# A two-layer SiLU block on one core: which queue loads the first slab of w1, and in what order the first tiles of x are transposed

## The chip, the cores and the metric

The kernel runs on one core of a Trainium2 chip. The metric is the device time of one execution in microseconds; the median of three runs of the kernel before is 124.64 us (124.32 to 124.81). Its profile is of one further execution on the same core.

## The reference

`x` is 2048 x 640, `w1` 640 x 1728, `w2` 1728 x 640, all bf16. The kernel computes

```python
h = jnp.einsum("bsd,df->bsf", x, w1)
h = _silu(h)
out = jnp.einsum("bsf,fd->bsd", h, w2)
```

## The kernel before

**Tiling.** The 640 rows of w1 are five slabs of 128 (index k), held in SBUF as `w1s[:, k, :]`. The 1728 columns are 13 blocks of 128 and a last one of 64. x is needed with its 640 columns on the partitions, so it is loaded by transposing DMAs into `xT[:, k, :]`; a "tile" here is 128 columns of x (one k) by one chunk of 512 rows, and there are four chunks. A block of h for one chunk is the sum over the five k of a matmul of slab k's block with tile k. Each such matmul is issued as a pair of 64 columns of weights (`step`, L183 to L187), whose two halves stand beside each other in the array; a pair is called a part. ScalarE applies SiLU as it moves a finished block from PSUM to SBUF (L179). The second product, with w2, follows when all of h is there.

**The opening.** For the first chunk, the first eight blocks have one PSUM bank each. So the loop order is turned round there: for each k in turn, one sweep over the eight blocks (`sweep`, L192 to L195; eight parts each). Sweep k needs slab k of w1 (its first 1024 columns, 256 KB) and tile k of x, and nothing else, so that TensorE can begin when the first slab and the first tile are there and the others arrive behind. The fifth sweep (L208 to L211) finishes the blocks. After it come the other five blocks of the first chunk, whose columns are loaded separately as `ld_rest` and `ld_rest2` (L156, L157), then the three other chunks, whose 15 one-tile transposing loads (L163) and the loads of w2 follow on the same queue.

**Ahead of the opening** TensorE runs dummy matmuls on a zeroed tile `z` (L129 to L138): 13 over the full array and then one pair of 64 columns, each 256 wide. Their result is overwritten.

**Queues.** The helper `early` (L98 to L109) moves an instruction ahead of the barrier at the program's head, at the end of what already stands there for the same engine, so that on each engine the order of the `early` calls is the order of issue. SyncE's order is written out by hand in L123 and L148 to L157: tiles 0 and 1 in one transposing load; the last three of slab 0's eight blocks; slab 1; slab 2; tile 2; slab 3; tiles 3 and 4 in one load; slab 4; the two loads of the remaining columns. ScalarE issues one load, the first five blocks of slab 0 (L124, `NA = 5`), and then warms up its SiLU table (L144). Each load has a semaphore of its own, and TensorE waits at the head of each sweep for the loads that it needs (L199, L205, L208), and once more inside sweep 0, at block 5, for the last three blocks (L202). All transposing loads are issued from SyncE.

Of the kernel before, what the change touches and what calls it, by code (L numbers as in the profile page):

```python
# [9 lines left out]
def bass_standalone__dense_activation_silu__prompt_kernel(  # L10
# [13 lines left out]
    P = 128  # L24
    NB = 8
    BANK = 512
    DT = D // P
    FT = F // P
    FL = F - FT * P
    SCH = 512  # L30
# [8 lines left out]
    pe, act, dve, pool, sp = nc.tensor, nc.scalar, nc.vector, nc.gpsimd, nc.sync  # L39

    with ExitStack() as es:
# [18 lines left out]
        def sem(name):  # L60
            s = es.enter_context(nc.semaphore(name))
            count[s.name if hasattr(s, "name") else name] = 0
            return [s, 0]

        def tick(ins, s, n=1):
            ins.then_inc(s[0], n)
            s[1] += n
            return (s, s[1])

        def wait(eng, *points):  # L70
            for pt in points:
                if pt is None:
                    continue
                s, v = pt
                key = (id(eng), id(s))
                if seen.get(key, 0) < v:
                    eng.wait_ge(s[0], v)
                    seen[key] = v
# [6 lines left out]
        def load(eng, out_ap, in_ap):  # L85
            s = sem(f"s_ld{n_dma[0]}")
            n_dma[0] += 1
            return tick(eng.dma_start(out=out_ap, in_=in_ap), s, 16)

        def turned(c0, c1, k0, k1):  # L90
            s = sem(f"s_tr{n_dma[0]}")
            n_dma[0] += 1
            return tick(sp.dma_start_transpose(
                out=xT[:, k0:k1, c0:c1], in_=xf[c0:c1, k0 * P:k1 * P]), s, 16)

        ET = mybir.EngineType

        def early(emit, engine, arrived=True):  # L98
            n = len(nc.main_func.blocks[0].instructions)
            r = emit()  # L100
            lst = nc.main_func.blocks[0].instructions
            new = lst[n:]
            del lst[n:]
            at = next(
                i for i, ins in enumerate(lst)
                if ins.opcode == ("EventSemaphore" if arrived else "Drain") and ins.engine == engine
            )
            lst[at:at] = new
            return r  # L109
# [2 lines left out]
        w2_v = w2[0:F0, :].rearrange("(ft p) d -> p ft d", p=P)  # L112

        NO = NB
        NA = 5
        CO = NO * P

        def slab(eng, k, f0=0, f1=NO):
            return load(eng, w1s[:, k, f0 * P:f1 * P], w1_v[:, k, f0 * P:f1 * P])

        ld_w1 = {}
        ld_t = {}
        ld_t[0] = ld_t[1] = early(lambda: turned(0, SCH, 0, 2), ET.SP, False)  # L123
        ld_w1[0] = early(lambda: slab(act, 0, 0, NA), ET.Activation, False)  # L124
        p_z = early(lambda: tick(dve.memset(z[:, :], 0.0), s_dve), ET.DVE, False)  # L125

        bank_free = [None] * NB
# [1 line left out]
        def dummies(n, w):  # L129
            for _ in range(n):  # L130
                for c0 in range(0, P, w):
                    pe.matmul(ps[c0:c0 + w, 3, 0:HB], lhsT=z[:, 0:w], rhs=z[:, :],  # L132
                              start=True, stop=True)

        def first_dummies():
            wait(pe, p_z)
            dummies(13, P)
            dummies(1, HC)  # L138

        p_warm = early(lambda: tick(pool.memset(warm[:, :], 0.0), s_pool), ET.Pool, False)  # L140
# [4 lines left out]

        early(warm_up, ET.Activation, False)

        ld_w1b = early(lambda: slab(sp, 0, NA, NO), ET.SP, False)  # L148
        ld_w1[1] = early(lambda: slab(sp, 1), ET.SP, False)
        ld_w1[2] = early(lambda: slab(sp, 2), ET.SP, False)  # L150
        ld_t[2] = early(lambda: turned(0, SCH, 2, 3), ET.SP, False)
        ld_w1[3] = early(lambda: slab(sp, 3), ET.SP, False)
        ld_t[3] = ld_t[4] = early(lambda: turned(0, SCH, 3, DT), ET.SP, False)
        ld_w1[4] = early(lambda: slab(sp, 4), ET.SP, False)
        CM = CO + 2 * P
        ld_rest = early(lambda: load(sp, w1s[:, :, CO:CM], w1_v[:, :, CO:CM]), ET.SP, False)  # L156
# [32 lines left out]
        def part(k, ft, c0, c1, start=False, stop=False):  # L189
            return step(ft, k, ft, c0, c1, start, stop)  # L190

        def sweep(k, c0, c1, *waits):  # L192
            wait(pe, *waits)
            for ft in range(NO):
                part(k, ft, c0, c1)  # L195

        def opening():
            first_dummies()
            wait(pe, ld_t[0], ld_w1[0])  # L199
            for ft in range(NO):  # L200
                if ft == NA:
                    wait(pe, ld_w1b)  # L202
                part(0, ft, 0, SCH, start=True)
            for k in range(1, DT - 1):
                sweep(k, 0, SCH, ld_w1[k], ld_t[k])  # L205

        early(opening, ET.PE)
        wait(pe, ld_w1[4], ld_t[4])  # L208
        for ft in range(NO):
# [198 lines left out]
```

## Time and profile before

| what | value |
|---|---|
| median of three runs (lowest, highest) | 124.64 us (124.32, 124.81) |
| span of the profiled execution | 123.84 us (123.8 on the page) |
| its distance to the median of the runs | 0.80 us |
| TensorE matmuls busy | 121.3 us, 98% of the span |
| TensorE weight loads busy | 58.9 us, 48% |
| ScalarE, VectorE, GpSimd busy | 38.8, 6.9, 0.3 us |
| DMA packets | 10.42 MB, mean 84 GB/s |

The profile has a page, which gives busy times, the chain of work that ended last, the costliest groups and the DMA issues, and a trace behind it that can be asked further: a timeline in order of time, the same for one engine, the transfers with the time from issue to landing, and busy times in stretches of the span. Engines are named PE (matmuls), PEld (weight loads, which overlap the matmuls), ACT (ScalarE), DVE (VectorE), POOL (GpSimd) and SP (SyncE); SPq and ACTq are the DMA issues of SyncE and ScalarE. Times count from the span's start. In a line such as "3.82 0.18 PEld L175 ... [0.42 <-DMA xT<-in_x_dram]" the first number is the start, the second the length of what is merged there, "x4" the number of instructions, and the bracket the idle time just before with what ended it. The profiled execution is one among several, and the runs differ among themselves by up to 0.5 us.

### The profile page before, as it was taken

The numbers are of one execution on the slowest core, as the hardware profiler recorded it, in microseconds if no ns is written. First come the engines' busy times: TensorE is split into PE (matmuls) and PEld (weight loads), VectorE is DVE, ScalarE is ACT, GpSimd is POOL, SyncE is SP. The second block draws the span as 40 slices with busy tenths as digits, with TensorE's granted clock in tenths as the row PEclk, the third lists the DMA queues.
The fourth block names the chain that finished last, engine by engine and source line by source line (L and its number), as shares of the span: only waits on it lengthen the run. The fifth ranks groups of instructions, "written<-read, shape, count | busy, mean of one in ns | idle before, by whom it ended". The sixth has DMA issues, their size and how long they took to land.

```text
span 123.8 us, 2298 instructions
## 1 busy us (share of the span) xinstructions
PE 121.3 (98%) x1056; PEld 58.9 (48%) x1057; DVE 6.9 (6%) x11; ACT 38.8 (31%) x67; POOL 0.3 (0%) x5
## 2 busy tenths in 40 slices
PE   8999999999999999999999999999999999999993
PEld 5345545545545545545544444444444444444452
DVE  0000000000000000000000022002200300222001
ACT  4000985555555555555530011001100200110110
POOL 0000000000000000000000000000000000000000
DMA  6999974554894000000000004302200220023112
GB/s 138 239 246 331 138 86 91 100 77 107 214 394 157 0 0 0 3 5 0 0 0 5 0 0 101 74 0 105 107 0 5 106 106 0 5 106 116 53 66 82
DMA packets 19625, 10.42 MB, mean 84 GB/s; under 512 B 13728, under 2 KB 19104, under 8 KB 19616
## 3 DMA queue, kind: packets, MB, share of 16 engines
q1 hardware_dynamic: 19472, 10.11, 34.1%
q10 hardware_dynamic: 144, 0.16, 0.6%
q8 instruction: 8, 0.13, 0.5%
q14 instruction: 1, 0.01, 0.0%
HBM read 4.51 MB, written 2.62 MB: 58 GB/s over the span
## 4 chain that ended last, share of the span: by engine, by line
PE 95%; DMA 3%; ACT 0%; issue 0%
PE ps L175 95%; DMA xT<-in_x_dram 3%; ACT o_sb L256 0%
## 5 line engine op out<-in xcount | busy, mean ns | idle before, releaser
L175 PE MATMUL ps<-xT,w1s 128*64 128x512 bf16 x540 | 59.6, 384 | 0.1
L175 PE MATMUL ps<-w2s,hT 64*128 64x512 bf16 (+3 forms) x376 | 46.0, 369 | 0.2 <-issue 0.2
L175 PEld LDWEIGHTS ps<-xT,w1s 128*64 128x64 bf16 x540 | 30.0, 111 | 29.6 <-issue 1.2
L179 ACT ACTIVATE hT<-ps 128x512 bf16<-128x512 f32 x52 | 30.0, 607 | 29.9 <-PE ps L175 29.9
L175 PEld LDWEIGHTS ps<-w2s,hT 64*128 64x128 bf16 (+1 forms) x377 | 21.0, 95 | 24.2 <-issue 0.2
L256 ACT CAST o_sb<-ps 128x512 bf16<-128x512 f32 (+1 forms) x9 | 5.0, 551 | 41.5 <-PE ps L175 41.5
L175 PE MATMUL ps<-hT,w2s 64*128 64x512 bf16 x104 | 11.7, 376 | 0.0
L175 PEld LDWEIGHTS ps<-hT,w2s 64*128 64x128 bf16 x104 | 5.0, 94 | 6.3 <-issue 0.4
L254 DVE CAST o_sb<-ps 128x512 bf16<-128x512 f32 (+1 forms) x8 | 5.4, 675 | 40.5 <-PE ps L175 40.5
L254 DVE CAST oT<-ps 128x512 bf16<-128x512 f32 x2 | 1.4, 692 | 74.2 <-PE ps L175 74.2
L256 ACT CAST oT<-ps 128x512 bf16<-128x512 f32 x2 | 1.2, 586 | 10.6 <-PE ps L175 10.6
L132 PE MATMUL ps<-z 128*128 128x256 bf16 (+1 forms) x15 | 3.3, 419 | 0.4 <-DVE z L125 0.4
L175 PE MATMUL ps<-w2t,hTt 64*128 64x512 bf16 (+2 forms) x17 | 2.9, 363 | 0.0
L132 PEld LDWEIGHTS ps<-z 128*128 128x128 bf16 (+1 forms) x15 | 1.9, 142 | 1.5 <-issue 0.4
L179 ACT ACTIVATE hTt<-ps 128x512 bf16<-128x512 f32 x2 | 1.2, 598 | 1.0 <-PE ps L175 1.0
L144 ACT ACT_TABLE_LOAD x1 | 1.3, 1283 | 0.5 <-issue 0.5
L175 PEld LDWEIGHTS ps<-w2t,hTt 64*128 64x128 bf16 x17 | 0.9, 94 | 1.1
L175 PE MATMUL ps<-hTt,w2t 64*128 64x512 bf16 x4 | 0.8, 376 | 0.0
L175 PEld LDWEIGHTS ps<-hTt,w2t 64*128 64x128 bf16 x4 | 0.2, 94 | 0.2
L144 ACT ACTIVATE warm<-warm 128x32 f32<-128x32 f32 x1 | 0.2, 229 | 0.0
L125 DVE MEMSET z<- 128x128 uint32 x1 | 0.2, 165 | 0.2 <-issue 0.2
L140 POOL MEMSET warm<- 128x32 f32 x1 | 0.1, 125 | 0.0
(4 smaller groups left out, 0.4 us busy)
## 6 DMA issues: line engine op xcount, KB each, us to landing
out_dram<-o_sb SPq DMA_DIRECT2D x15, 160.0 KB, 1.8
w2s<-in_w_dram SPq DMA_DIRECT2D x1, 1120.0 KB, 6.1
w1s<-in_w_dram SPq DMA_DIRECT2D x4, 256.0 KB, 4.1
w2s<-in_w_dram SPq DMA_DIRECT2D x1, 960.0 KB, 8.2
w1s<-in_w_dram SPq DMA_DIRECT2D x1, 560.0 KB, 7.0
w1s<-in_w_dram SPq DMA_DIRECT2D x1, 320.0 KB, 5.8
xT<-in_x_dram SPq DMA_TRANSPOSE x18, 3.7
w1s<-in_w_dram ACTq DMA_DIRECT2D x1, 160.0 KB, 2.7
```

Source lines behind the costliest of these rows:

```text
L125: p_z = early(lambda: tick(dve.memset(z[:, :], 0.0), s_dve), ET.DVE, False)
L132: pe.matmul(ps[c0:c0 + w, 3, 0:HB], lhsT=z[:, 0:w], rhs=z[:, :], start=True, stop=True)
L140: p_warm = early(lambda: tick(pool.memset(warm[:, :], 0.0), s_pool), ET.Pool, False)
L144: act.activation(out=warm[:, :], in_=warm[:, :], func=ACT.Silu)
L175: return pe.matmul(o, lhsT=l, rhs=r, start=start, stop=stop, skip_group_check=shared)
L179: r = tick(act.activation(out=out_ap, in_=in_ap, func=ACT.Silu), s_act)
L254: r = tick(dve.tensor_copy(out=out_ap, in_=in_ap), s_dve)
L256: r = tick(act.copy(out=out_ap, in_=in_ap), s_act)
```

## The change

ScalarE loads all eight blocks of slab 0 in one load. SyncE no longer loads a part of it. The two-tile load of tiles 0 and 1 at the head of SyncE's queue becomes a load of tile 0 alone; tiles 1 and 2 follow in one load, then slabs 1 and 2, then tiles 3 and 4 in one load, slab 3, slab 4 and the remaining columns as before. The number of transposing loads stays at three. TensorE's wait inside sweep 0 goes, and there is one full-array dummy fewer, 12 in place of 13.

```diff
-        NA = 5
...
-        ld_t[0] = ld_t[1] = early(lambda: turned(0, SCH, 0, 2), ET.SP, False)
-        ld_w1[0] = early(lambda: slab(act, 0, 0, NA), ET.Activation, False)
+        ld_t[0] = early(lambda: turned(0, SCH, 0, 1), ET.SP, False)
+        ld_w1[0] = early(lambda: slab(act, 0), ET.Activation, False)
...
-            dummies(13, P)
+            dummies(12, P)
             dummies(1, HC)
...
-        ld_w1b = early(lambda: slab(sp, 0, NA, NO), ET.SP, False)
+        ld_t[1] = ld_t[2] = early(lambda: turned(0, SCH, 1, 3), ET.SP, False)
         ld_w1[1] = early(lambda: slab(sp, 1), ET.SP, False)
         ld_w1[2] = early(lambda: slab(sp, 2), ET.SP, False)
-        ld_t[2] = early(lambda: turned(0, SCH, 2, 3), ET.SP, False)
+        ld_t[3] = ld_t[4] = early(lambda: turned(0, SCH, 3, 5), ET.SP, False)
         ld_w1[3] = early(lambda: slab(sp, 3), ET.SP, False)
-        ld_t[3] = ld_t[4] = early(lambda: turned(0, SCH, 3, DT), ET.SP, False)
         ld_w1[4] = early(lambda: slab(sp, 4), ET.SP, False)
...
             wait(pe, ld_t[0], ld_w1[0])
             for ft in range(NO):
-                if ft == NA:
-                    wait(pe, ld_w1b)
                 part(0, ft, 0, SCH, start=True)
```

## The prediction

> **What bounds the kernel now.** I read four views: the chain of waits, the timeline of the first 14 us, the landing times of single transfers, and the table of stretches (busy times, DMA share and GB/s, us by us).
>
> The chain first, by share and then in order of time (start us, us, what):
>
> ```profile
> PE 95%; DMA 3%; ACT 0%; issue 0%
> PE ps L175 95%; DMA xT<-in_x_dram 3%; ACT o_sb L256 0%
> ```
>
> ```profile
> 0.00 3.78 DMA xT<-in_x_dram
> 3.78 0.04 issue
> 3.82 106.78 PE ps L175 x706
> ```
>
> TensorE sets the end from 3.82 us on, without a break until 110 us. So the change can act in two ways: through the 3.78 us ahead of the first real matmul, and through a stall or a change of rate inside the opening, where sweep k needs slab k of w1 and tile k of x. Everything after the opening moves along with it, one for one.
>
> The timeline of the weight loads (start us, us, engine, line) gives TensorE's pace there:
>
> ```profile
> 0.39 2.48 PEld L132 LDWEIGHTS ps<-z 128*128 128x128 bf16 x13 [0.39 <-DVE z L125]
> 3.27 0.13 PEld L132 LDWEIGHTS ps<-z 128*64 128x64 bf16 x2 [0.41 <-issue]
> 3.82 0.18 PEld L175 LDWEIGHTS ps<-xT,w1s 128*64 128x64 bf16 x4 [0.42 <-DMA xT<-in_x_dram]
> 4.25 0.18 PEld L175 LDWEIGHTS ps<-xT,w1s 128*64 128x64 bf16 x2 [0.25 <-issue]
> ...
> 5.53 0.18 PEld L175 LDWEIGHTS ps<-xT,w1s 128*64 128x64 bf16 x2 [0.25 <-DMA w1s<-in_w_dram]
> 5.96 0.18 PEld L175 LDWEIGHTS ps<-xT,w1s 128*64 128x64 bf16 x2 [0.25 <-issue]
> 6.30 7.67 PEld L175 LDWEIGHTS ps<-xT,w1s 128*64 128x64 bf16 x72 [0.17 <-issue]
> ```
>
> A part is a pair of 64-column matmuls. Up to 5.96 us a pair comes every 0.427 us; from 6.30 on, 72 loads (36 pairs) take 7.67 us, or about 0.216 us a pair with the edges. TensorE therefore runs at half pace until about 6.2 us: the mixed step of 0.34 us holds x at the slow pace with x + 0.216(1 - x/0.427) = 0.34, so x = 0.25 and the change comes at 5.96 + 0.25 = 6.21. (The granted clock in the stretches by stage reads 1.00 all the while, so it does not show this; the pace does.) One consequence carries the sum: **while that moment stays where it is, 1 us of earlier start is worth only 1 - 0.216/0.427 = 0.494 us**, since each pair done early is done at the slow price.
>
> The pair at 5.96 is the sixth, so sweep 0 ends with pairs at 6.30 and 6.52, and sweeps 1 to 4 begin at 6.73, 8.46, 10.18 and 11.91 (8 pairs of 0.216 us each), the remaining columns at 13.64.
>
> SyncE's issues (start us, us to issue):
>
> ```profile
> 0.00 1.33 SPq L93 DMA_TRANSPOSE xT<-in_x_dram  x1
> 1.39 1.54 SPq L88 DMA_DIRECT2D w1s<-in_w_dram  x3
> 2.97 1.16 SPq L93 DMA_TRANSPOSE xT<-in_x_dram  x1
> 4.17 0.58 SPq L88 DMA_DIRECT2D w1s<-in_w_dram  x1
> 4.79 1.24 SPq L93 DMA_TRANSPOSE xT<-in_x_dram  x1
> 6.07 1.62 SPq L88 DMA_DIRECT2D w1s<-in_w_dram  x3
> ```
>
> A transposing load costs 1.16 us to issue with one tile and 1.24 or 1.33 with two: nearly the same. The three at 1.39 begin at 1.39, 2.00 and 2.49. Asked one by one in narrow windows, the transfer view gives issue to landing (last number of its lines):
>
> ```profile
> xT<-in_x_dram SPq DMA_TRANSPOSE x1, 3.8
> w1s<-in_w_dram ACTq DMA_DIRECT2D x1, 160.0 KB, 2.7
> w1s<-in_w_dram SPq DMA_DIRECT2D x1, 96.0 KB, 3.9
> ```
>
> The first tiles so land at 3.8, ScalarE's part of slab 0 at 0.12 + 2.7 = 2.8, the rest of it at 5.3. In the same way slabs 1 and 2 land at 5.9 and 6.6, tile 2 at 7.15, slab 3 at 8.25, tiles 3 and 4 at 9.2, slab 4 at 10.55, the rest of the columns at 12.5 and 14.15. Each is 0.65 us or more ahead of the pair that needs it: after 3.82 no transfer stops TensorE now.
>
> **The change part by part.**
>
> *One dummy fewer.* The 13 full ones are 0.213 us apart (0.39 to 2.93). The last pair of dummies starts at 3.27 and leaves TensorE free at about 3.49; with 12 at 3.27. It costs nothing and gains nothing so long as the data come after 3.27; that is the floor of the new start.
>
> *The start.* It now needs tile 0 and the whole of slab 0. Tile 0: lower bound, a lone one-tile transpose issued at 17.80 landed after 2.9 us; upper bound, the 3.8 us of the two-tile load. Slab 0: at least 2.8; its 96 KB more (98 kB) at the 248 GB/s that the stretch 2 to 3 us moved are 0.40 us, so 3.2; upper bound 0.12 + 4.1 = 4.2 by the 256 KB slabs, which had others ahead of them. If the two transfers did not disturb each other, the start would be the floor, 3.27. If the engines were full, only the swap would count: a one-tile transpose less (tile 2 landed 0.56 us behind slab 2 on the same queue) against 0.40 us more, 0.16 us net: 3.66. The stretch 1 to 2 us has a DMA share of 0.70 against 1.25 in the next, so there is some room: I take the middle, **3.45**, 0.37 earlier, worth 0.37 x 0.494 = **0.18 us**.
>
> The Trainium skill, "DMA: Bandwidth & Descriptors", section "Issuing engines are not separate DMA queues", speaks against the change: transfers issued on different engines run on the same 16 DMA engines and interleave, so that a second issuer saves the issue time alone. By that rule the start would be the full-engine bound; this trace agrees in so far as two tiles beside 160 KB took 3.8 us where a lone tile took 2.9.
>
> *The wait that goes (ft = 5).* Its load landed at 5.3, ahead of the pair at 5.96; the 0.25 us idle in the row at 5.53 is the same as in the rows that waited for "issue". Nothing gained.
>
> *The order on SyncE.* The 96 KB issue goes (0.6 us); the two-tile load for 1 and 2 comes in its place at 1.39 and lasts to 2.63. Behind it are queued: slab 1 now issued at 2.69 (was 2.00), slab 2 at 3.2 (2.49), tiles 3 and 4 at 3.7 (4.79), slab 3 at 5.0 (4.17), slab 4 at 5.6 (6.07), the rest at 6.2 and 6.7, the later chunks 0.6 us sooner. Landings, by what stands ahead on the queue: tiles 1 and 2 at 1.39 + 3.8 = 5.2 at the latest. Slab 1 has one tile more ahead than now (0.56 us), the 96 KB counted as still ahead because they share the engines: 5.9 + 0.56 = **6.45**; bounds 5.9 (no delay) and 2.69 + 4.5 = 7.2 (the slowest 256 KB slab, slab 4). Slab 2: 7.15. Tiles 3 and 4: one step of 1.0 (9.2 - 8.25) on, 8.15. Slab 3: 9.2. Slab 4 and the rest: no later than now.
>
> *Who needs them.* With the start at 3.45 sweep 0 ends at 6.73 - 0.18 = 6.55, and sweeps 2 to 4 begin at 8.28, 10.0 and 11.73. The margins: slab 1 0.10 us, slab 2 1.1, slab 3 0.8, slab 4 1.2, the rest 0.95. Slab 1 is next in line: its margin shrinks from 0.85 us to almost nothing.
>
> *Sum.* The profiled span is 123.84 us; it becomes 123.66. The median of the runs, 124.64, lies 0.80 us above that span; I carry the difference over: **124.46**. A measurement of this kernel can tell about 0.5% (0.62 us) from no change.
>
> **The rivals.**
>
> *B, the engines are full, so the change does not do what it says.* Start at 3.66, gain 0.16 x 0.494 = 0.08: 124.56. For it: the DMA share of 1.25. Against: the 0.70 before.
>
> *C, slab 1 becomes the wait.* It lands between 6.55 and 7.2, sweep 1 starts there instead of at 6.73, and all behind it moves by the difference: from -0.18 to +0.45, so 124.5 to 125.1. For it: the issue 0.69 us later and the tiny margin. Against: the slab had 0.85 us to spare, and tiles 1 and 2 are ready to flow as soon as tile 0 is through.
>
> *D, slower: the full pace comes later.* The start loses one dummy, and a slab 0 that lands late (up to 4.2) would leave TensorE idle from 3.27 for 0.9 us. If that gap restarts what leads to the full pace, then, as now 5.8 us passed from the first dummy (0.39) to 6.21, it would come at 4.2 + 5.8 = 10.0, 3.8 us later, worth 3.8 x 0.494 = 1.9, and the start itself 0.4: up to 126.9; half of that, 125.8, as its middle. It decides only if slab 0 lands clearly behind 3.8. Against: the gap of 0.33 us now (3.49 to 3.82) did no such thing.
>
> *E, faster: the full pace comes sooner.* If it comes a fixed time after the real start, the gain is 0.37, 124.27; if the gap alone holds it back, sooner still. But slab 1 then stops the gain: sweep 1 can't start before 6.45, or 5.9 by its best bound, so -0.28 or -0.83: 124.35 to 123.8.
>
> The Trainium skill, "TensorE: Matmul & The Clock Gate", Part 1, says that the window which releases the full clock (3.4 us there) runs freely, unlinked to the kernel's start; by that the moment varies between runs alike for both kernels, and neither D nor E follows from the edit. The trace has one such moment, 6.21, and can't tell.
>
> **How the numbers follow.** Forecast (start 3.3 to 3.6, no stall over 0.1 us): 0.46. B: 0.12. C: 0.22. D: 0.10. E: 0.10. Beyond 0.5% lie D and a fifth of C on the slow side (0.14) and most of E with a little of the forecast on the fast side (0.10); the rest, 0.76, is no change. The range takes in C to 125.1 and E to near its limit, with the runs' own spread (124.32 to 124.81): 123.95 to 125.2.
>
> **What would show it.** The chain of the changed kernel should begin with a transfer that ends near 3.4 (tile 0 or slab 0) in place of 3.78; weight loads 0.43 us apart up to about 6.2; no idle time of PEld put down to w1s near 6.5. A wait there for slab 1 is C; loads 0.43 apart beyond 7 us are D; before 5.5 only, E. The forecast is wrong if the first matmul starts after 3.8 or the moment of full pace moves by over a microsecond.

## The result, and the profile after

The changed kernel takes 125.05 us (median of 12 runs, 124.69 to 126.79), the kernel before 124.42 in its 12 runs of the same measurement (123.90 to 124.81): ratio 1.005, interval 1.003 to 1.007. It is **slower by about 0.6 us**. Ratios here leave out executions more than 1.5% above a kernel's fastest, two at 126.8 us in this case; medians hold all runs.

The chain of the changed kernel, by share and in order of time:

```profile
PE 95%; DMA 3%; ACT 0%; issue 0%
PE ps L173 95%; DMA xT<-in_x_dram 3%; ACT o_sb L252 0%
```

```profile
0.00 3.84 DMA xT<-in_x_dram
3.84 0.04 issue
3.88 106.36 PE ps L173 x976
```

The chain still begins with tile 0's transfer, and it is one tile now, yet it ends no sooner: 3.84 in place of 3.78. The weight loads of the opening:

```profile
3.06 0.13 PEld L131 LDWEIGHTS ps<-z 128*64 128x64 bf16 x2 [0.41 <-issue]
3.88 0.18 PEld L173 LDWEIGHTS ps<-xT,w1s 128*64 128x64 bf16 x4 [0.69 <-DMA xT<-in_x_dram]
4.32 0.18 PEld L173 LDWEIGHTS ps<-xT,w1s 128*64 128x64 bf16 x2 [0.25 <-issue]
4.74 0.18 PEld L173 LDWEIGHTS ps<-xT,w1s 128*64 128x64 bf16 x2 [0.25 <-issue]
5.17 0.83 PEld L173 LDWEIGHTS ps<-xT,w1s 128*64 128x64 bf16 x8 [0.25 <-issue]
6.35 7.70 PEld L173 LDWEIGHTS ps<-xT,w1s 128*64 128x64 bf16 x74 [0.35 <-DMA w1s<-in_w_dram]
```

Two things differ from before. The pace doubles at 5.3 us (the step after 5.17 is a mixed one) and not at 6.2. And at the head of sweep 1 the weight loads stop for slab 1, until 6.35. These loads run ahead of the matmuls, so their 0.35 us of idle time is not what the matmuls lose. The matmuls have no break there:

```profile
3.88 10.42 PE L173 MATMUL ps<-xT,w1s 128*64 128x512 bf16 x88 [0.40 <-DMA xT<-in_x_dram]
```

Sweep 0's last pair starts at 6.10, so the next could have started at 6.32; it starts at 6.35. In this execution the wait for slab 1 costs 0.03 us, a near tie. The transfers, first of tile 0, then of tiles 1 and 2 (issued at 1.29), then of slab 1 (issued at 2.62):

```profile
xT<-in_x_dram SPq DMA_TRANSPOSE x1, 3.8
xT<-in_x_dram SPq DMA_TRANSPOSE x1, 3.6
w1s<-in_w_dram SPq DMA_DIRECT2D x1, 256.0 KB, 3.7
```

Slab 1 lands at 2.62 + 3.7 = 6.3, and the wait of the weight loads ends there.

**A riddle first.** This profile's span, 123.48 us, is shorter than the 123.84 of the profile before, though the kernel is slower. The executions of the changed kernel list both their time and their span: 124.80 and 123.5 for the profiled one, 1.3 us apart in each. If as much lies outside the span before, the profile that the prediction was built on belongs to an execution of about 125.15 us, longer than all 12 of its runs. A second profile of the same kernel (the run e7 below) settles this:

> The kernel before once more, for a second profile. By the times, its usual execution is 0.6 us shorter than that of the changed kernel, and the span outside is alike, so sweep 1 should begin near 6.0 here, not at 6.73: full pace before the sixth pair, slab 1 landed by 5.9 and no wait after sweep 0. If the pace again changes at 6.2 and sweep 1 begins at 6.7, the moment of full pace is a property of this kernel, and the times must differ for another reason.

It took 124.37 us with a span of 123.03 (1.34 apart):

```profile
3.67 0.19 PEld L175 LDWEIGHTS ps<-xT,w1s 128*64 128x64 bf16 x4 [0.26 <-DMA xT<-in_x_dram]
4.10 0.18 PEld L175 LDWEIGHTS ps<-xT,w1s 128*64 128x64 bf16 x2 [0.24 <-issue]
4.53 0.44 PEld L175 LDWEIGHTS ps<-xT,w1s 128*64 128x64 bf16 x4 [0.24 <-issue]
5.18 0.43 PEld L175 LDWEIGHTS ps<-xT,w1s 128*64 128x64 bf16 x6 [0.22 <-DMA w1s<-in_w_dram]
5.81 7.14 PEld L175 LDWEIGHTS ps<-xT,w1s 128*64 128x64 bf16 x68 [0.20 <-DMA w1s<-in_w_dram]
```

Here the pace doubles near 4.75 us, the matmuls of sweep 1 begin at 5.93, and slab 1 landed at 5.77, 0.16 us ahead of them; their weight loads already wait for it (the row at 5.81), without delaying them. In the first profile it had 0.85 us to spare only because that execution reached full pace at 6.2.

One number then orders the profiles that have full pace and no wait behind it: the moment at which sweep 1 begins. The rest of the span is 117.1 us each time: 6.73 and 123.84, 5.93 and 123.03 before; 6.35 and 123.48 after; 6.27 and 123.39, 7.66 and 124.8 in e6 and e4 below.

This lets the listed spans of executions that were not profiled be read too, as an estimate: span less 117.1. The executions of the changed kernel other than the two at 126.8 us have spans of 123.4 to 124.0, so sweep 1 began at about 6.3 to 6.9, in the middle near 6.55. Of the 26 executions of the kernel before beside e1 to e4, 18 have spans of 122.8 to 123.3, so 5.7 to 6.2. The changed kernel has lost the early ones. Slab 1's landing explains such a floor: 5.77 and 5.88 in the two profiles before, 6.30 after and 6.57 in e3 below.

### The profile page after: what moved, and what is told of

The parts are those of the page before. It is cut to its first block, busy times and chain, and to the rows that moved or that the text cites. A ratio compares the mean times of both kernels' runs of the same rounds, so it can differ in the third digit from the quotient of the medians.

```text
span 123.5 us, 2295 instructions
## 1 busy us (share of the span) xinstructions
PE 120.7 (98%) x1055; PEld 59.5 (48%) x1056; DVE 7.0 (6%) x11; ACT 38.8 (31%) x67; POOL 0.3 (0%) x5
## 3 DMA queue, kind: packets, MB, share of 16 engines
HBM read 4.51 MB, written 2.62 MB: 58 GB/s over the span
## 4 chain that ended last, share of the span: by engine, by line
PE 95%; DMA 3%; ACT 0%; issue 0%
PE ps L173 95%; DMA xT<-in_x_dram 3%; ACT o_sb L252 0%
## 5 line engine op out<-in xcount | busy, mean ns | idle before, releaser
L173 PEld LDWEIGHTS ps<-xT,w1s 128*64 128x64 bf16 x540 | 30.7, 111 | 28.7 <-issue 0.7
```

The source lines that it names most:

```text
L173: return pe.matmul(o, lhsT=l, rhs=r, start=start, stop=stop, skip_group_check=shared)
```

## The experiments

The theory: sweep 1 begins when sweep 0 is done, slab 1 is there and tile 1 is there; the change puts tile 2 and the larger first load ahead of them on shared DMA engines, and so takes away what an early full pace would give. The rivals: the idle stretch ahead of the first real matmul, which delays the full pace; the whole slab on ScalarE by itself; the extra or moved issues on SyncE. In the expectations the "slab theory" and the "theory of sweep 1's needs" are this theory; the "gap theory" and the "theory of idle and pace" are the first rival. Medians of the kernel before beside them are 124.49 (e1 to e4), 124.55 (e5, e6, e8) and 124.45 (e9 to e12).

**e1: slab 1 ahead of tiles 1 and 2.**

```diff
-        ld_t[1] = ld_t[2] = early(lambda: turned(0, SCH, 1, 3), ET.SP, False)
         ld_w1[1] = early(lambda: slab(sp, 1), ET.SP, False)
+        ld_t[1] = ld_t[2] = early(lambda: turned(0, SCH, 1, 3), ET.SP, False)
```

> The changed kernel with slab 1 issued ahead of the load of tiles 1 and 2. Slab theory (in the changed kernel sweep 1 waits for slab 1, which lands at 6.30, behind two tiles): slab 1 lands near 5, tiles 1 and 2 near 5.7, no wait at the head of sweep 1, and the median falls by 0.3 to 0.6 us against the changed kernel, to 124.4 to 124.75 against a kernel before at 124.4. Gap theory (what costs is the idle stretch of 0.6 us ahead of the first real matmul, which delays the full pace; the slab wait only takes up what the pace would have lost): first matmul still at 3.85 or later and the median stays within 0.15 us of 125.05.

125.15 us, ratio to before 1.0042 (1.0019 to 1.0066). Slab 1 lands at 5.5, but tiles 1 and 2 only at 6.5, and sweep 1 begins at 6.62. The gain expected was not there: one needed load was exchanged for another, with the same 128 KB too much ahead. The gap theory is not supported either, since the first matmul came at 3.73, 0.15 earlier, without any gain.

**e2 and e4: the two parts alone**, on the kernel before. e2:

```diff
-        NA = 5
...
-        ld_w1[0] = early(lambda: slab(act, 0, 0, NA), ET.Activation, False)
+        ld_w1[0] = early(lambda: slab(act, 0), ET.Activation, False)
...
-        ld_w1b = early(lambda: slab(sp, 0, NA, NO), ET.SP, False)
...
-                if ft == NA:
-                    wait(pe, ld_w1b)
```

> The kernel before with one part of the change alone: ScalarE loads the whole slab 0, SyncE the tiles as before (0 and 1 in one load), slab 1 next. Slab theory: slab 1 is issued at 1.39 in place of 2.00 and lands at 5.2 to 5.9, so no wait; first matmul where it was, 3.8 to 3.9; the median is that of the kernel before within 0.15 us, or up to 0.2 us less. If loading the whole slab on ScalarE were itself the cost (slab 0 later than the tiles): first matmul after 4.0 and the median 0.1 to 0.4 us above the kernel before.

125.31 us, five of twelve runs above 126.5, the others from 124.28; ratio 1.0036 (1.0011 to 1.0062). In its profile, of one of the long runs, the two tiles land at 4.26 where they landed at 3.63 and 3.78: the 96 KB more on the other queue hold them back 0.5 to 0.6 us. So this part costs by itself, against the slab theory's expectation. e4:

```diff
-        ld_t[0] = ld_t[1] = early(lambda: turned(0, SCH, 0, 2), ET.SP, False)
+        ld_t[0] = early(lambda: turned(0, SCH, 0, 1), ET.SP, False)
...
         ld_w1b = early(lambda: slab(sp, 0, NA, NO), ET.SP, False)
+        ld_t[1] = ld_t[2] = early(lambda: turned(0, SCH, 1, 3), ET.SP, False)
         ld_w1[1] = early(lambda: slab(sp, 1), ET.SP, False)
         ld_w1[2] = early(lambda: slab(sp, 2), ET.SP, False)
-        ld_t[2] = early(lambda: turned(0, SCH, 2, 3), ET.SP, False)
-        ld_w1[3] = early(lambda: slab(sp, 3), ET.SP, False)
         ld_t[3] = ld_t[4] = early(lambda: turned(0, SCH, 3, DT), ET.SP, False)
+        ld_w1[3] = early(lambda: slab(sp, 3), ET.SP, False)
```

> The kernel before with the other part of the change alone: tile 0 by itself, then the last three blocks of slab 0, tiles 1 and 2 in one load, slabs 1 and 2, tiles 3 and 4, slab 3, slab 4; ScalarE's share of slab 0 and the 13 dummies as before. Slab theory: slab 1 now stands behind two tiles and 96 KB, lands at 6.4 to 6.8 and sweep 1 waits for it; median 0.4 to 0.9 us above the kernel before. Gap theory: with 96 KB between the two transposing loads tile 0 lands at 3.1 to 3.4, the gap closes, and the median is at or below the kernel before.

126.12 us (four runs), ratio 1.012 (1.009 to 1.0149): 1.6 us above before, more than either theory expected, since slab 1 lands at 7.62 and not by 6.8. Tile 0 lands at 3.14 and the first matmul stands directly behind the dummies, an earlier start than in any profile so far, and yet:

```profile
3.30 0.37 PEld L175 LDWEIGHTS ps<-xT,w1s 128*64 128x64 bf16 x4
...
7.66 5.32 PEld L175 LDWEIGHTS ps<-xT,w1s 128*64 128x64 bf16 x52 [1.43 <-DMA w1s<-in_w_dram]
```

An early start with a late slab 1 is worth nothing: sweep 1 stands until 7.66.

**e3: two more dummies in the changed kernel.**

```diff
-            dummies(12, P)
+            dummies(14, P)
```

> The changed kernel with 14 full dummies in place of 12, so that TensorE is idle for 0.15 us and not 0.6 ahead of the first real matmul. Gap theory: the full pace comes sooner and the runs over 126 do not occur; the median falls by 0.3 to 0.6 us. Slab theory: sweep 1 still begins when slab 1 has landed, near 6.3, so the median stays at 125.05 within 0.2 us, with the runs over 126 gone at most.

125.11 us, ratio 1.0046 (1.0029 to 1.0062), one of twelve runs at 126.7. The time stays, as the slab theory has it. In the profile the full pace comes at 5.1 and sweep 0 would let sweep 1 begin at 6.40; slab 1 (6.57) holds it until 6.62, 0.22 us this time:

```profile
6.62 6.40 PEld L173 LDWEIGHTS ps<-xT,w1s 128*64 128x64 bf16 x62 [0.54 <-DMA w1s<-in_w_dram]
```

The idle stretch was hardly shortened here, though: tile 0 landed at 4.17 in this execution, so the weight loads stood for 0.59 us where they stood for 0.69. The run says little against the gap theory.

**e6: tile 2 ahead of slab 1, in the kernel before.**

```diff
+        ld_t[2] = early(lambda: turned(0, SCH, 2, 3), ET.SP, False)
         ld_w1[1] = early(lambda: slab(sp, 1), ET.SP, False)
         ld_w1[2] = early(lambda: slab(sp, 2), ET.SP, False)
-        ld_t[2] = early(lambda: turned(0, SCH, 2, 3), ET.SP, False)
```

> The kernel before with one line moved: the load of tile 2 goes ahead of slab 1; everything else as before. Theory of sweep 1's needs: slab 1 lands 0.5 to 0.9 us later (6.4 to 6.8), sweep 1 waits for it, and the median rises by 0.4 to 0.8 us over the kernel before. Theory of the whole slab on ScalarE: no change beyond 0.15 us.

125.21 us, ratio 1.0037 (1.0022 to 1.0053), 0.66 above before. This profile has the full pace nearly from the start, so that sweep 0 is done at 5.6, and the gain is lost to slab 1, which lands at 6.22, a little earlier than expected. Here the matmuls do have a break, the last row; sweep 1 begins 0.7 us later than sweep 0 would allow:

```profile
3.65 0.19 PEld L175 LDWEIGHTS ps<-xT,w1s 128*64 128x64 bf16 x4 [0.25 <-DMA xT<-in_x_dram]
4.05 1.19 PEld L175 LDWEIGHTS ps<-xT,w1s 128*64 128x64 bf16 x12 [0.22 <-issue]
6.26 3.16 PEld L175 LDWEIGHTS ps<-xT,w1s 128*64 128x64 bf16 x32 [1.02 <-DMA w1s<-in_w_dram]
```

```profile
6.27 7.10 PE L175 MATMUL ps<-xT,w1s 128*64 128x512 bf16 x64 [0.54 <-DMA w1s<-in_w_dram]
```

One moved line makes a loss as large as the whole change's, with ScalarE's load and the dummies untouched. The twelve runs lie in two groups, five at 124.66 to 124.75 and seven at 125.18 to 125.34. The profile is of the lower group, and what holds the upper one back by another 0.5 us was not seen.

**e5 and e8: tile 1 alone.** e5 is the changed kernel with

```diff
-        ld_t[1] = ld_t[2] = early(lambda: turned(0, SCH, 1, 3), ET.SP, False)
+        ld_t[1] = early(lambda: turned(0, SCH, 1, 2), ET.SP, False)
         ld_w1[1] = early(lambda: slab(sp, 1), ET.SP, False)
         ld_w1[2] = early(lambda: slab(sp, 2), ET.SP, False)
-        ld_t[3] = ld_t[4] = early(lambda: turned(0, SCH, 3, 5), ET.SP, False)
+        ld_t[2] = early(lambda: turned(0, SCH, 2, 3), ET.SP, False)
         ld_w1[3] = early(lambda: slab(sp, 3), ET.SP, False)
+        ld_t[3] = ld_t[4] = early(lambda: turned(0, SCH, 3, 5), ET.SP, False)
```

> The changed kernel with tile 1 loaded alone where it loads tiles 1 and 2, tile 2 behind slab 2, and slab 3 ahead of tiles 3 and 4, as before. Theory of sweep 1's needs (sweep 1 begins when slab 1 and tile 1 have both landed, and everything that is put ahead of them on the DMA engines, tile 2 in the change, delays that): slab 1 lands at 5.6 to 5.9 in place of 6.3 to 6.6, and the median falls by 0.3 to 0.6 us from 125.05 toward the kernel before. Theory that what costs is the load of the whole slab 0 on ScalarE (it delays tile 0): the first matmul stays at 3.8 or later and the median stays within 0.15 us of 125.05. Issue cost (a transposing load more on SyncE, 1.25 us): a wait at sweep 3 for tiles 3 and 4 of up to 0.4 us would eat a part.

126.31 us: a miss in the time, though slab 1 did land at 5.6. Three runs took 124.4 to 125.1, one 125.9, eight 126.1 to 127.1. The profile is of a long one:

```profile
4.21 0.18 PEld L174 LDWEIGHTS ps<-xT,w1s 128*64 128x64 bf16 x4 [1.02 <-DMA xT<-in_x_dram]
...
8.90 0.18 PEld L174 LDWEIGHTS ps<-xT,w1s 128*64 128x64 bf16 x2 [0.25 <-issue]
9.28 3.78 PEld L174 LDWEIGHTS ps<-xT,w1s 128*64 128x64 bf16 x36 [0.20 <-issue]
```

The weight loads stood for 1.0 us ahead of the first real one (the matmuls for 0.7), and TensorE kept half pace until 9.2. That is another mechanism than slab 1, and the rival of the idle stretch comes back as a second cost. In e8 ScalarE issues the five and the three blocks in two loads, SyncE the tiles as in e5, with 13 dummies:

```diff
-        ld_t[0] = ld_t[1] = early(lambda: turned(0, SCH, 0, 2), ET.SP, False)
+        ld_t[0] = early(lambda: turned(0, SCH, 0, 1), ET.SP, False)
...
+        ld_w1b = early(lambda: slab(act, 0, NA, NO), ET.Activation, False)
...
-        ld_w1b = early(lambda: slab(sp, 0, NA, NO), ET.SP, False)
+        ld_t[1] = early(lambda: turned(0, SCH, 1, 2), ET.SP, False)
```

> ScalarE issues slab 0 in two loads, five blocks and then three; SyncE tile 0 alone, tile 1 alone, slabs 1 and 2, tile 2, slab 3, tiles 3 and 4, slab 4; 13 dummies. Theory of sweep 1's needs: nothing that sweep 0 or 1 does not need stands ahead, slab 1 lands at 5.5 to 5.9, tile 0 with 160 KB beside it at first at 3.2 to 3.5; the median is 0 to 0.4 us below the kernel before. If the extra transposing issue or the shared engines cost more, 0.1 to 0.5 us above it, with a wait at sweep 1 or 3.

125.00 us, three runs above 126.7; ratio 1.0034 (1.0021 to 1.0048): 0.45 above before, as the second of the expectations has it. Tile 0 lands at 4.4, not by 3.5. What splitting the load did to it one profile does not tell: e5 and e9 below have the same loads, and their tile 0 lands at 4.16 and 3.62. Sweep 3 waits 0.24 us for tiles 3 and 4 (landed at 9.73). The profiled execution had full pace from its first real matmul, after an idle stretch as long as e5's. Its trace shows why: the last two dummy matmuls took 0.31 and 0.32 us, where they took 0.42 in every other profile, so the pace had doubled already during them, near 3.5 us, ahead of the stretch.

**e9, e10, e11: the idle stretch by itself.** e9 is e5 with 16 dummies in place of 12, e10 is e2 with 16 in place of 13, e11 the kernel before with 10 in place of 13.

> The changed kernel with tile 1 alone (as in the run with that edit, 126.31 us, where the pace stayed at half until 9.1 us) and 16 full dummies in place of 12, which end at 4.1 us and leave no idle stretch of 0.9 us ahead of the first real matmul. Theory of idle and pace (an idle stretch of 0.8 us or more ahead of the first real matmul lets the full pace come 3.4 us later): no run above 126, full pace by 6.4 us at the latest. Theory of sweep 1's needs: slab 1 at 5.6 then lets sweep 1 begin near 6.0, and the median is 124.3 to 124.8, level with the kernel before. If the extra transposing load were the cost: still above 125 with no long slow stretch.

> The kernel before with the whole slab 0 on ScalarE (125.31 us, five of twelve runs above 126.5) and 16 dummies in place of 13. Theory of idle and pace: no run above 126; the first matmul stays near 4.2 to 4.3 since the tiles land there; slab 1 near 5.9; median 124.4 to 125.0. If the runs above 126 came from something else: as many of them as without the dummies.

> The kernel before with 10 dummies in place of 13 and nothing else changed: TensorE is then idle from 2.85 to about 3.7, 0.8 to 0.95 us. Theory of idle and pace: a part of the runs, a third or more, lies 1.3 to 2 us above the others, at 126 or more, with half pace until 8 us or later in them; the others stay at 124.5. If idle time ahead of the start has no such effect: all runs within 0.3 us of the kernel before.

e9: 124.82 us, highest 125.16; ratio 1.0030 (1.0015 to 1.0045). e10: 124.76, highest 125.38; 1.0026 (1.0005 to 1.0048). e11: 126.45 (six runs, four of them above 126.4); 1.013 (1.009 to 1.017). Three dummies taken from the kernel before cost 2.0 us. Three added to e2 and four to e5 take 0.55 and 1.5 us off the medians, and no run above 126 is left; by the ratios the gain is only 0.1 and 0.4 us, within their intervals, so what the dummies take away is mainly the long runs. The profile of e11:

```profile
3.73 0.19 PEld L175 LDWEIGHTS ps<-xT,w1s 128*64 128x64 bf16 x4 [0.96 <-DMA xT<-in_x_dram]
...
8.85 0.18 PEld L175 LDWEIGHTS ps<-xT,w1s 128*64 128x64 bf16 x2 [0.25 <-issue]
9.23 3.78 PEld L175 LDWEIGHTS ps<-xT,w1s 128*64 128x64 bf16 x36 [0.21 <-issue]
```

In e9, where the stretch is filled, the full pace comes by 6.0 and no wait stands at sweep 1. But the dummies now hold the first matmul to 4.13, while tile 0 landed at 3.62:

```profile
3.94 0.37 PEld L174 LDWEIGHTS ps<-xT,w1s 128*64 128x64 bf16 x4
...
5.84 7.25 PEld L174 LDWEIGHTS ps<-xT,w1s 128*64 128x64 bf16 x68 [0.25 <-issue]
```

**e12: tile 0 alone without the two costs**, from the kernel before: tile 0, the last three blocks, slab 1, tile 1, slab 2, tile 2, tiles 3 and 4, slab 3, slab 4.

```diff
-        ld_t[0] = ld_t[1] = early(lambda: turned(0, SCH, 0, 2), ET.SP, False)
+        ld_t[0] = early(lambda: turned(0, SCH, 0, 1), ET.SP, False)
...
         ld_w1[1] = early(lambda: slab(sp, 1), ET.SP, False)
+        ld_t[1] = early(lambda: turned(0, SCH, 1, 2), ET.SP, False)
...
-        ld_w1[3] = early(lambda: slab(sp, 3), ET.SP, False)
         ld_t[3] = ld_t[4] = early(lambda: turned(0, SCH, 3, DT), ET.SP, False)
+        ld_w1[3] = early(lambda: slab(sp, 3), ET.SP, False)
```

> A version that keeps tile 0 alone and avoids both costs: ScalarE five blocks of slab 0; SyncE tile 0, the last three blocks, slab 1, tile 1 alone, slab 2, tile 2, tiles 3 and 4, slab 3, slab 4; 13 dummies. No transposing load directly behind tile 0, nothing ahead of slab 1 that sweep 1 does not need. Tile 0 lands at 3.1 to 3.3 and the first matmul follows at 3.3 without idle time; slab 1 at 5.3 to 5.8, tile 1 at 5.5 to 6.0. Theory of sweep 1's needs: sweep 1 begins at 5.6 to 6.1, median 124.1 to 124.6, at or a little below the kernel before; a wait at sweep 3 for slab 3 (issued at 6.7) of up to 0.3 us may take the gain. If tile 1 behind slab 1 lands after 6.4: 125 or more.

125.65 us (six runs), ratio 1.0093 (1.0064 to 1.0122): a miss. Sweep 1 indeed begins at 5.7, the earliest of all profiles; the gain is then lost twice, to tile 2 (landed at 7.98) and to slab 3 (issued at 6.84, landed at 10.84):

```profile
5.70 1.47 PEld L176 LDWEIGHTS ps<-xT,w1s 128*64 128x64 bf16 x16 [0.28 <-issue]
8.09 1.47 PEld L176 LDWEIGHTS ps<-xT,w1s 128*64 128x64 bf16 x16 [0.92 <-issue]
10.88 2.08 PEld L176 LDWEIGHTS ps<-xT,w1s 128*64 128x64 bf16 x22 [1.33 <-DMA w1s<-in_w_dram]
```

A fourth transposing issue on SyncE (1.1 to 1.4 us each) pushes what stands behind it, and here tiles 3 and 4 stand ahead of slab 3 as well; the two were not tried apart. No version tried beats the kernel before.

## Why the prediction was wrong

The forecast was 0.18 us faster; measured, 0.6 us slower. Two steps failed: the moment at which sweep 1 begins, taken as 6.73 from one profile, and the start, taken as 0.37 us earlier. The mechanism that was named for the slow side is rival C, with a chance of 0.22. That the measured 125.05 lies at C's upper end is luck: C reached it with slab 1 at 7.2, while slab 1 landed at 6.3 and the base lay lower.

1. *The base.* The step that failed first: "The margins: slab 1 0.10 us" and "its margin shrinks from 0.85 us to almost nothing", and with it the sum on the span of 123.84 us and the 0.80 us carried over. Outside the span lie 1.3 us, not 0.8, so the profile was of an execution 0.7 us longer than usual, with full pace at 6.2. In the second profile the pace doubles at 4.75, sweep 1 begins at 5.93, and slab 1 has 0.16 us to spare. The landing itself was well predicted (6.45, bounds 5.9 to 7.2; it was 6.30), but it is 0.4 us late by that profile, not on time.

2. *The start.* Predicted 3.45, with 3.66 as the bound "if the engines were full"; it was 3.88, beyond the 3.8 that the prediction gave as a sign of being wrong. The error is in tile 0's bounds, 2.9 to 3.8, and in counting the added 96 KB as 0.16 us net. With 160 KB beside it a lone tile 0 lands at 3.14 (e4) and 2.89 (e12), with 256 KB at 3.69 (e1): the load that was moved costs 0.55 us and more, what the halved transfer gains. The rule of the Trainium skill that the prediction set beside this ("DMA: Bandwidth & Descriptors", section "Issuing engines are not separate DMA queues": the loads of all issuers run on the same 16 engines and interleave) agrees with these rows; B, worked along it, was still too kind by 0.22 us.

3. *The price of the start.* An earlier start with the moment of full pace fixed is worth 0.216/0.427 = 0.506 of itself, not 1 less that, 0.494; at half pace the two are nearly alike, and 0.18 becomes 0.19. (0.494 is what a later full pace costs, of itself.) D counted its later start in full (0.4) where by the same price half goes: 126.7, not 126.9.

4. *The dummy.* "It costs nothing" holds for an execution that gets its full pace anyway. But the 0.69 us of idle loads is nearer to the point where the pace slips: 2 of 12 runs took 126.8 us, about what D's later pace would cost (neither was profiled), and e11 shows that mechanism in the kernel before. The other ten runs, at 124.69 to 125.27, are not of this kind: the profiled one had its full pace at 5.3.

5. *The wait at ft = 5* and the landings of slab 2 and later (7.0, 8.05, 8.9 against 7.15, 8.15, 9.2) were right: no wait behind sweep 1 in the profile after.

6. *The size.* Between the profile after and the second one before, sweep 1 begins 0.42 us later. Of this the wait for slab 1 is 0.03; by the prices above the later start (3.88 against 3.67) is 0.11 and the later full pace (5.3 against 4.75), which differs as much between executions of one kernel, is 0.27. So this pair of profiles alone does not show slab 1 as the cause. What speaks for it is the lost early executions, e3, where it holds the matmuls up for 0.22 us, and e6, where tile 2 ahead of slab 1 costs 0.66 us by itself. From the changed kernel, moving tile 2 out of slab 1's way and covering the idle stretch gives 124.82 (e9), 0.23 to 0.29 below the change (125.05) and e3 (125.11). The 0.37 us that remains against before is no longer slab 1 (5.86 in e9): in its profile sweep 1 begins at 6.72, because the dummies hold the start to 4.13 and the full pace comes at 5.9. The whole slab on ScalarE with the stretch covered costs 0.31 us (e10), there by a start that waits for the tiles until 4.21. These act through the same moment, the beginning of sweep 1, and the latest sets it; how the 0.6 us divides among them is not shown.

## What the runs showed of the hardware

*The pace of TensorE.* The moment of full pace differs between executions of one kernel: 6.2 and 4.75 us in two profiles of the kernel before. With 0.69 us of idle loads or less ahead of the first real matmul it came by 6.4 us in every profile; with 0.89, 0.96 and 1.02 (e2, e11, e5) at 8.7 to 9.2, and with 1.03 in e8 it had already come, near 3.5 us, ahead of the stretch. The granted clock reads 1.00 throughout. The Trainium skill, "TensorE: Matmul & The Clock Gate", Part 1, describes a window of 3.4 us that runs freely; after at least one busy window the clock is released. This fits the spread without a slip (3.5 to 6.4 us over all profiles) and the slip to 8.7 to 9.2. No run shows the window itself, nor how busy it must be: the changed kernel and e3, with 0.69 and 0.59 us in their profiles, also had three runs at 126.7 to 126.8 that were not profiled. What of the median loss in step 6 comes from chance in that moment stays open, since each kernel has one profile or two.

*A transposing load behind another.* Each load's completion comes as 16 increments. Tile 0's lay within 0.13 to 0.15 us of each other where a plain load followed it (e1, e4, e12), and 0.24 to 0.93 us apart where a transposing load did (the change 3.30 to 3.84, e3, e5, e8, e9). TensorE waits for the last. Why, the traces do not say, and it was not tried apart.

## What to carry to other kernels

Before building a sum on one profile, check that its execution is a usual one: its own time against the median, or a second profile; a margin of 0.85 us was one of 0.16. Read a wait from the matmuls, not from the weight loads that run ahead of them: 0.35 us of idle loads were 0.03 us of the time. Where loads share the DMA engines, order them by who needs them next, and count everything put ahead of the second need, not only of the first: an earlier start is worth nothing if the next operand comes late enough (e4). Keep the matrix engine busy up to the first real matmul; three dummies too few cost 2 us here.
